# Splitting the first transposes' PSUM tile in two, so that ScalarE and VectorE copy its halves out side by side

## The chip, the cores and the metric

One NeuronCore of a Trainium2 chip runs the whole program. The metric is the device time of one execution in microseconds (us); lower is better. The spans quoted with traces run from the first to the last instruction and are about 1.7 us shorter than the time.

## The reference

Two layers are applied twice, with residual adds, to x of 2048 tokens by 1024 features in bf16:

```python
x = A_x
x = x + A(layernorm(x))     # 32 heads, window of 8 keys with dilation 2, then @ wo
x = x + B(layernorm(x))     # relu(x W_gate) * (x W_up) @ W_down, F = 3584
x = x + A(layernorm(x))
x = x + B(layernorm(x))
```

The kernel works on blocks of 512 tokens (four token tiles of 128). Only its first 15 us matter here: load block 0 of x, normalise it, transpose it so that features lie on partitions (`xnT`), and start the V projection `x @ wqkv[:, 2048:3072]` of that block.

## The kernel before

Tile 0 and 1 are normalised on VectorE; tile 2's statistics run on ScalarE at the same time. TensorE transposes a token tile in eight 128x128 pieces into one PSUM tile `tp` (128 partitions by 2 KB, one bank), and two engines copy it to SBUF, VectorE the first four pieces (`xnT[:, t, 0:4]`) and ScalarE the last four. `on("v", ...)` and `on("a", ...)` keep each engine's instructions in the order written.

```python
        def turn(t):
            tps[t] = psum.tile([P, KC, P], BF16, tag="acc", name="tp")
            for c in range(KC):
                with pe_group():
                    tail_pe[0] = nc.tensor.transpose(tps[t][:, c, :], xna[:, t, c * P:(c + 1) * P], ident[:]).ins

        def copy(t, eng, c0=0, c1=KC):
            f = nc.vector.tensor_copy if eng == "v" else nc.scalar.copy
            on(eng, f, hold["xnT"][:, t, c0:c1, :], tps[t][:, c0:c1, :])

        warm = small("warm")
        on("a", nc.scalar.activation, warm[:], ones[:, 0:1], ACT.Identity)
        scratch(14)                # 14 matmuls on ones, only to warm TensorE up
        # [cut: statistics of tiles 0 and 1 on VectorE, of tile 2 on ScalarE]
        apply(0)                   # normalise, VectorE
        turn(0)
        apply(1)
        copy(0, "v", 0, KC // 2)
        copy(0, "a", KC // 2, KC)
        turn(1)
        act_vpe(2, st1)            # three small VectorE operations for tile 2
        copy(1, "v", 0, KC // 2)
        copy(1, "a", KC // 2, KC)
        # [cut: statistics of tile 3; tiles 2 and 3 are turned and copied later, between V matmuls]
```

The V matmuls of block 0 take token tiles 0 and 1 first (256 columns), accumulating over eight feature chunks `kc`. The first four chunks need VectorE's halves, the last four ScalarE's:

```python
        plan = [(c, 0, 2) for c in range(6)] + [(c, 2, 4) for c in range(6)] + [(c, 0, 4) for c in range(6, KC)]
        # for each (c, t0, t1): for kc in range(8):
        mm(acc[:, cols], lhsT=slab[("v0", c // 4)][:, kc, (c % 4) * P:(c % 4 + 1) * P],
           rhs=ln["xnT"][:, t0:t1, kc, :], start=(kc == 0), stop=(kc == KC - 1))
```

Weights arrive in slabs of 1 MB through a ring of five; the first V slab is the fourth transfer in the SyncE queue, behind three transfers of x:

```python
        def f(key=key, src=src):
            shp = list(src.shape)
            t = wring.tile([P, 8 * SLAB], BF16, tag="slab", name=...)
            tv = t[:, 0:shp[1] * shp[2]].rearrange("p (a b) -> p a b", b=shp[2])
            sp_dma(tv, src)
            slab[key] = tv
```

## Time and profile before

| | before |
|---|---|
| time, median of the first three runs, none of them profiled | 1630.64 us (1630.27 to 1630.65) |
| profiled execution | 1630.08 us, span 1628.4 us |
| TensorE busy | 1618.6 us, 99% of the span |
| first V matmul starts | 9.69 us |
| fifth V matmul starts | 10.30 us |

This is the view of TensorE's waits of the kernel before: who waited, for whom, total us, times, longest.

```profile
PE scratch L129 <- DVE ones L296: 1.5, 1, 1.5
PE dacc L129 <- DVE x L700: 0.8, 1, 0.8
PE acc_v L129 <- DVE xnT_first L103: 0.6, 1, 0.6
PE tp L364 <- DVE xn_first L103: 0.4, 1, 0.4
```

There is nothing else in 1628 us. A change to the first transposes can act only on the third line and on what comes just after it.

Next, lines of the timeline of the kernel before, by engine: start, duration, instruction, shape, and in brackets the idle time before it and what ended it. PE is TensorE, DVE is VectorE, ACT is ScalarE.

```profile
7.45 0.62 PE L364 MATMUL tp<-ident,xn_first 128*128 128x128 bf16 x8
7.83 0.55 DVE L103 TENSOR_SCALAR xn_first<-x,mv,rstd 128x1024 bf16<-128x1024 bf16 x1 [0.45 <-POOL rstd L314]
8.30 0.42 DVE L103 COPY xnT_first<-tp 128x512 bf16<-128x512 bf16 x1
8.44 0.62 PE L364 MATMUL tp<-ident,xn_first 128*128 128x128 bf16 x8 [0.37 <-DVE xn_first L103]
...
8.75 0.58 ACT L314 COPY xnT_first<-tp 128x512 bf16<-128x512 bf16 x1 [1.62 <-DVE xnT_first L103]
...
9.22 0.41 DVE L103 COPY xnT_first<-tp 128x512 bf16<-128x512 bf16 x1
...
9.67 0.58 ACT L314 COPY xnT_first<-tp 128x512 bf16<-128x512 bf16 x1 [0.34 <-DVE xnT_first L103]
9.69 2.96 PE L129 MATMUL acc_v<-xnT_first,w_v 128*128 128x256 bf16 x24 [0.63 <-DVE xnT_first L103]
9.69 0.42 PEld L129 LDWEIGHTS <-w_v 128*128 128x128 bf16 x4 [0.75 <-issue]
10.30 2.06 PEld L129 LDWEIGHTS <-w_v 128*128 128x128 bf16 x19 [0.20 <-issue]
```

Read the two ScalarE lines. ScalarE sat idle for 1.62 us and started its copy at 8.75, just after VectorE's copy of the same token tile had ended (8.30 + 0.42). It did the same at 9.67. The two engines take turns on one PSUM tile. The last two lines (PEld) are TensorE's weight loads: four at 9.69, then a pause to 10.30, when the fifth V matmul starts. ScalarE's second half is ready just before (9.67 + 0.58).

The Trainium skill, page "PSUM — Partial Sum Buffer", section "PSUM bank collisions raise a hardware error", says that two engines must not access one bank on the same 32 partitions at once, reads included, and that the hardware does not arbitrate. So the order has to be kept by waits, and this trace shows them kept: never both engines on one tile. That the target in SBUF is not the cause is visible too: VectorE's copy of tile 1 (from 9.22) runs while ScalarE still copies tile 0 (to 9.33).

### The profile page before, as it was taken

The numbers are of one execution on the slowest core, as the hardware profiler recorded it, in microseconds if no ns is written. First come the engines' busy times: TensorE is split into PE (matmuls) and PEld (weight loads), VectorE is DVE, ScalarE is ACT, GpSimd is POOL, SyncE is SP. The second block draws the span as 40 slices with busy tenths as digits, with TensorE's granted clock in tenths as the row PEclk, the third lists the DMA queues.
The fourth block names the chain that finished last, engine by engine and source line by source line (L and its number), as shares of the span: only waits on it lengthen the run. The fifth ranks groups of instructions, "written<-read, shape, count | busy, mean of one in ns | idle before, by whom it ended". The sixth has DMA issues, their size and how long they took to land.

```text
span 1628.4 us, 18703 instructions
## 1 busy us (share of the span) xinstructions
PE 1618.6 (99%) x7589; PEld 782.2 (48%) x7638; DVE 1062.6 (65%) x926; ACT 506.1 (31%) x1050; POOL 255.7 (16%) x220
## 2 busy tenths in 40 slices
PE   9999999999999999999999999999999999999999
PEld 6644445444544445444454444544445444444444
DVE  5799899985497927949179492894818958211211
ACT  4754313243241513405134051331513311131110
POOL 2421003310250102201052010520105100000000
PEclk9999999999999999999999999999999999999999
DMA  9579656746476485664857647577484764655451
GB/s 303 93 203 252 167 177 199 192 156 200 136 215 175 155 233 171 184 175 150 229 181 185 187 150 225 162 203 212 151 231 154 194 205 155 206 164 172 156 168 65
DMA packets 371463, 296.83 MB, mean 182 GB/s; under 512 B 142512, under 2 KB 351664, under 8 KB 370480
## 3 DMA queue, kind: packets, MB, share of 16 engines
q1 hardware_dynamic: 371088, 295.23, 63.2%
q8 instruction: 60, 0.98, 0.3%
q10 hardware_dynamic: 288, 0.39, 0.1%
q14 instruction: 27, 0.22, 0.0%
HBM read 256.77 MB, written 21.00 MB: 171 GB/s over the span
## 4 chain that ended last, share of the span: by engine, by line
PE 95%; DVE 4%; issue 1%; DMA 0%; POOL 0%; DVEq 0%
PE acc_g L129 24%; PE acc_u L129 24%; PE dacc L129 22%; PE acc_v L129 7%; PE acc_k L129 6%; PE acc_q L129 6%; PE acc_wo L129 6%; DVE t L541 2%; DVE ac L551 1%; PE L L129 1%; DVE pv L603 0%; DVE x L648 0%; DVE pv L604 0%; DVE ac L541 0%; DMA x<-in_A_x_dram 0%
## 5 line engine op out<-in xcount | busy, mean ns | idle before, releaser
L129 PE MATMUL acc_g<-xnT_b,w_g 128*128 128x512 bf16 x1792 | 423.4, 379 | 0.0
L129 PE MATMUL acc_u<-xnT_b,w_u 128*128 128x512 bf16 x1792 | 423.3, 379 | 0.0
L129 PE MATMUL dacc<-w_d,hT 128*128 128x512 bf16 x1759 | 386.5, 379 | 2.5 <-DVE x L700 0.8
L672 ACT ACTIVATE r<-acc_g 128x512 bf16<-128x512 f32 x224 | 133.4, 596 | 747.1 <-PE acc_g L129 746.0
L673 DVE TENSOR_TENSOR hT<-acc_u,r 128x512 bf16<-128x512 f32 x224 | 153.7, 687 | 315.1 <-PE acc_u L129 313.5
L129 PEld LDWEIGHTS <-hT 128*128 128x128 bf16 x1792 | 175.4, 98 | 212.3 <-issue 1.0
L129 PEld LDWEIGHTS <-w_g 128*128 128x128 bf16 x1792 | 174.8, 98 | 212.7 <-issue 3.0
L129 PEld LDWEIGHTS <-w_u 128*128 128x128 bf16 x1792 | 175.4, 98 | 211.4
L541 DVE TENSOR_TENSOR t<-q,k 128x2048 f32<-128x2048 bf16 x84 | 191.7, 2290 | 8.6 <-ACT k L480 5.8
L551 DVE TENSOR_TENSOR ac<-ac,t 128x2048 f32<-128x2048 f32 x84 | 191.7, 2282 | 0.4
L485 POOL COPY kh<-k 128x14 bf16<-128x14 bf16 x64 | 81.2, 1273 | 471.9 <-ACT k L480 471.8
L700 DVE TENSOR_TENSOR x<-dacc,x 128x512 bf16<-128x512 f32 x64 | 42.5, 687 | 164.0 <-PE dacc L129 164.0
L603 DVE TENSOR_TENSOR pv<-a,vhm 128x4096 bf16<-128x4096 bf16 x64 | 145.2, 2282 | 0.0
L129 PE MATMUL acc_wo<-w_o,oT 128*128 128x512 bf16 x496 | 111.0, 379 | 0.8
L245 POOL TENSOR_TENSOR st_b<-st_b,neg_half 128x1 f32<-128x1 f32 x29 | 56.4, 1956 | 288.6 <-ACT st_b L244 288.6
L245 POOL TENSOR_TENSOR st_a<-st_a,neg_half 128x1 f32<-128x1 f32 x32 | 41.9, 1315 | 319.2 <-ACT st_a L244 319.1
L484 POOL COPY k<-kh 128x14 bf16<-128x14 bf16 x48 | 70.5, 1469 | 65.9 <-DVE t L541 43.8
L129 PEld LDWEIGHTS <-oT 128*128 128x128 bf16 x512 | 50.0, 98 | 60.4
L604 DVE TENSOR_TENSOR pv<-pv 128x2048 bf16<-128x2048 bf16 x64 | 77.4, 1215 | 0.2
L476 ACT CAST q<-acc_q 128x512 bf16<-128x512 f32 x64 | 37.3, 583 | 73.2 <-PE acc_q L129 73.2
L240 ACT ACTIVATE xn_b<-x 128x1024 bf16<-128x1024 bf16 x29 | 30.3, 1045 | 89.3 <-DVE x L648 89.3
L480 ACT CAST k<-acc_k 128x512 bf16<-128x512 f32 x64 | 37.3, 583 | 63.0 <-PE acc_k L129 62.8
(131 smaller groups left out, 1209.1 us busy)
## 6 DMA issues: line engine op xcount, KB each, us to landing
w_g<-in_B_W_gate_dram SPq DMA_DIRECT2D x56, 1024.0 KB, 7.0
w_u<-in_B_W_up_dram SPq DMA_DIRECT2D x56, 1024.0 KB, 5.4
w_d<-in_B_W_down_dram SPq DMA_DIRECT2D x48, 1024.0 KB, 5.8
w_o<-in_A_wo_dram SPq DMA_DIRECT2D x16, 1024.0 KB, 7.2
vhm<-v_d SPq DMA_DIRECT2D x32, 284.0 KB, 6.9
v_d<-vT SPq DMA_DIRECT2D x8, 1024.0 KB, 10.0
oT<-o_d SPq DMA_DIRECT2D x32, 256.0 KB, 4.4
w_d<-in_B_W_down_dram SPq DMA_DIRECT2D x16, 512.0 KB, 4.0
```

Source lines behind the costliest of these rows:

```text
L129: tail_pe[0] = nc.tensor.matmul(*args, **kwargs).ins
L245: nc.gpsimd.tensor_tensor(rstd, vpe, neg_half[:, 0:1], op=ALU.pow)
L476: tail_act[0] = nc.scalar.copy(q[:], acc[:]).ins
L484: nc.gpsimd.tensor_copy(k[:, 0:HALO], khalo[n - 1][:, c, :])
L485: nc.gpsimd.tensor_copy(khalo[n][:, c, :], k[:, BLK:BLK + HALO])
L541: nc.vector.tensor_tensor(t[:], i0, i1, op=ALU.mult)
L551: nc.vector.tensor_tensor(o, ac[:], t[:], op=ALU.add)
L603: nc.vector.tensor_tensor(tt[:], a_bc, v_sh, op=ALU.mult)
L604: nc.vector.tensor_tensor(tt[:, 0:4], tt[:, 0:4], tt[:, 4:8], op=ALU.add)
L672: tail_act[0] = nc.scalar.activation(r[:], acc[:], ACT.Relu).ins
L673: nc.vector.tensor_tensor(hold["hT"][:, j, :], accs["u"][:], r[:], op=ALU.mult)
L700: nc.vector.tensor_tensor(xs, ac[t], xs, op=ALU.add)
```

## The change

Each token tile gets two PSUM tiles of four pieces, in two banks, so the halves can be copied at the same time. The engines are also redistributed: both halves of tile 0 go to ScalarE, and the second half of tile 2 moves to VectorE.

```diff
         def turn(t):
-            tps[t] = psum.tile([P, KC, P], BF16, tag="acc", name="tp")
+            tps[t] = [psum.tile([P, KC // 2, P], BF16, tag="acc", name=f"tp{h}") for h in range(2)]
             for c in range(KC):
                 with pe_group():
-                    tail_pe[0] = nc.tensor.transpose(tps[t][:, c, :], xna[:, t, c * P:(c + 1) * P], ident[:]).ins
-
-        def copy(t, eng, c0=0, c1=KC):
+                    tail_pe[0] = nc.tensor.transpose(tps[t][c // (KC // 2)][:, c % (KC // 2), :],
+                                                     xna[:, t, c * P:(c + 1) * P], ident[:]).ins
+
+        def copy(t, eng, h):
             f = nc.vector.tensor_copy if eng == "v" else nc.scalar.copy
-            on(eng, f, hold["xnT"][:, t, c0:c1, :], tps[t][:, c0:c1, :])
+            on(eng, f, hold["xnT"][:, t, h * (KC // 2):(h + 1) * (KC // 2), :], tps[t][h][:])
 ... (cut)
-        copy(0, "v", 0, KC // 2)
-        copy(0, "a", KC // 2, KC)
+        copy(0, "a", 1)
+        copy(0, "a", 0)
         turn(1)
         act_vpe(2, st1)
-        copy(1, "v", 0, KC // 2)
-        copy(1, "a", KC // 2, KC)
+        copy(1, "v", 0)
+        copy(1, "a", 1)
 ... (cut)
-        hold["later"] = {2: (lambda: (turn(2), copy(2, "a"))),
-                         4: (lambda: (turn(3), copy(3, "v", 0, KC // 2), copy(3, "a", KC // 2, KC)))}
+        hold["later"] = {2: (lambda: (turn(2), copy(2, "a", 0), copy(2, "v", 1))),
+                         4: (lambda: (turn(3), copy(3, "v", 0), copy(3, "a", 1)))}
```

## The prediction

> **What bounds the kernel now.** TensorE. The page has PE busy 1618.6 of 1628.4 us (99%), and the view of waits lists only four PE waits in the whole run: 1.5 us for the first constant, 0.4 us for the second normalised token tile, 0.6 us before the first V matmul, 0.8 us near the end. So the change can act only on the start-up, before the first V matmul.
>
> **Start-up, from the timeline (us).** Transposes of tile 0 at 7.45, tile 1 at 8.44 (8 each, 0.61-0.62 together). DVE: normalise tile 1 at 7.83, copy (128x512) of tile 0 at 8.30, three small operations of tile 2's statistics at 8.63 to 9.15, copy of tile 1 at 9.22 (0.41). ACT: copies at 8.75 and 9.67 (0.58 each), each within 0.05 of the end of DVE's copy of the same tile, although ACT was free from 7.1. The first V matmul starts at 9.69; the fifth, which needs ACT's half, at 10.30 (0.17 later than its 0.109 step would give).
>
> ACT's copies are held because both halves lie in one PSUM tile, one bank. The Trainium skill, "PSUM — Partial Sum Buffer", section "PSUM bank collisions raise a hardware error", says two engines must not access one bank and quadrant at once, reads included. The trace agrees: never both on one tile. The SBUF target is not the cause: DVE's copy of tile 1 (9.22) overlaps ACT's of tile 0 (8.75 to 9.33).
>
> **What changes.** DVE's copy of tile 0 moves to ACT; tile 2's second half moves from ACT to DVE; the same-bank wait goes; four more PSUM slots are taken in the rotation of six.
>
> My new schedule, from those durations:
> - ACT copies tile 0: second half at 8.1, first at 8.6, done 9.18; tile 1's second half 9.10 to 9.69.
> - DVE: statistics from 8.30, tile 1's first half from 8.89 (its fourth transpose ends about 8.83, estimate from 0.219 each at 0.057 steps) to 9.31.
> - First V matmul at about 9.36 (was 9.69, gain 0.33); the fifth at 9.80, its data ready at 9.74, so the 0.17 stall goes too. Gain: 0.5 us.
>
> Later copies (tiles 2 and 3) were not waited for by PE before: nothing to gain there. PSUM rotation: each slot's previous user is, by this schedule, emptied over 1 us before it is asked for again, so no new PE wait.
>
> **Does the gain last?** PE runs on without waits for 1.6 ms, and the next weight slab and next x loads are issued when PE frees a slab (the DMA queue waited 10.9 us for PE there), so they move forward too. I expect all 0.5 us kept, or a tenth or two lost. That is 0.03%, about the width of the three runs (0.38 us).
>
> **Prediction:** 1630.15 us, range 1629.5 to 1630.75. Faster by over 2%: 0.005; within 2%: 0.99; slower by over 2%: 0.005.
>
> **What would show each step.** First V matmul 0.3 earlier, fifth 0.5 earlier; the PE wait before it about 0.3 instead of 0.6; ACT's and DVE's copies of tile 1 overlapping; first Q matmul at about 24.2 instead of 24.69; span 1627.9 instead of 1628.4.
>
> **What would make it wrong.** (1) DVE's half copy waits for all eight transposes: gain about 0.3. (2) ACT's copies start late or still serialise with DVE. (3) The slot rotation makes transposes or V matmuls wait for an eviction. (4) The early DMA, near saturated at 9 to 19 us, does not move with PE and a weight or x load is waited for at 25 to 60 us, giving the gain back. (5) A shifted DMA pattern that disturbs a later stage.

## The result, and the profile after

| | before | after |
|---|---|---|
| time, median (four runs each) | 1630.45 us (1630.27 to 1630.65) | 1630.44 us (1629.66 to 1630.48) |
| profiled execution, span | 1628.4 us | 1628.0 us |
| first V matmul | 9.69 us | 9.42 us |
| first Q matmul | 24.69 us | 24.24 us |
| last VectorE add | 1624.50 us | 1624.06 us |

Executions over 1.5% slower than the fastest of the same kernel are left out of the means. The ratio is 0.9999, with a 95% interval of 0.9981 to 1.0016. Such a ratio is the mean time of one kernel's runs over the mean of the other's of the same rounds, so it is not quite the ratio of the medians quoted.

The times do not differ, but the two traces do. These are the lines of the timeline after that answer to those of before.

```profile
7.42 0.62 PE L364 MATMUL tp<-ident,xn_first 128*128 128x128 bf16 x8 [0.37 <-DVE xn_first L103]
7.80 0.55 DVE L103 TENSOR_SCALAR xn_first<-x,mv,rstd 128x1024 bf16<-128x1024 bf16 x1 [0.45 <-POOL rstd L314]
8.07 1.58 ACT L314 COPY xnT_first<-tp 128x512 bf16<-128x512 bf16 x3 [0.86 <-PE tp L364]
8.27 0.15 DVE L103 TENSOR_SCALAR mean<-st 128x1 f32<-128x1 f32 x1
...
8.86 0.41 DVE L103 COPY xnT_first<-tp 128x512 bf16<-128x512 bf16 x1
...
9.39 2.53 PEld L129 LDWEIGHTS <-w_v 128*128 128x128 bf16 x24 [0.53 <-DMA w_v<-in_A_wqkv_dram]
9.42 2.78 PE L129 MATMUL acc_v<-xnT_first,w_v 128*128 128x256 bf16 x24 [0.39 <-DVE xnT_first L103]
```

ScalarE now starts at 8.07, released by the transposes and no longer by VectorE, and does three copies in a row; VectorE's copy of tile 1 (8.86 to 9.27) lies inside that stretch. The V matmuls run as one group of 24 in 2.78 us, where they took 2.96 us before: the pause before the fifth is gone. The weight load at 9.39 is labelled as released by the DMA of the slab `w_v`. In this trace that is loose, for the slab had landed at 8.9 (issued at 2.23, 6.7 to landing) and VectorE's copy ended later (9.27). The weight load comes equally late, 9.43, in after_half below, whose half slab had landed at 7.5; in both traces a separate wait for VectorE stands in TensorE's queue ahead of that weight load. Still, the label is a warning to keep in mind.

The chain that ended last shows where the gain goes: start and duration of each piece, here the first V matmuls, the first Q matmuls and the end. First the kernel before, then after.

```profile
10.30 2.34 PE acc_v L129 x20
...
24.85 1.73 PE acc_q L129 x8
...
1624.50 0.69 DVE x L700
```

```profile
9.42 2.78 PE acc_v L129 x24
...
24.40 1.73 PE acc_q L129 x8
...
1624.06 0.69 DVE x L701
```

The shift is 0.45 us at the first Q matmuls and 0.44 us at the last add, 1600 us later. In this pair of traces the whole gain arrives at the end. And yet the three other executions of the changed kernel, of which only times and spans exist, took 1630.44 to 1630.48 us, as long as before. The one low time of the four is the profiled one.

### The profile page after: what moved, and what is told of

It reads as the page before. It is cut to its first block, busy times and chain, and to the rows that moved or that the text cites. A ratio compares the mean times of both kernels' runs of the same rounds, so it can differ in the third digit from the quotient of the medians.

```text
span 1628.0 us, 18706 instructions
## 1 busy us (share of the span) xinstructions
PE 1618.0 (99%) x7589; PEld 782.0 (48%) x7638; DVE 1062.8 (65%) x926; ACT 506.3 (31%) x1051; POOL 256.0 (16%) x220
## 4 chain that ended last, share of the span: by engine, by line
PE 95%; DVE 4%; issue 1%; DMA 0%; POOL 0%; DVEq 0%
PE acc_g L129 24%; PE acc_u L129 24%; PE dacc L129 22%; PE acc_v L129 7%; PE acc_k L129 6%; PE acc_q L129 6%; PE acc_wo L129 6%; DVE t L542 2%; DVE ac L552 1%; PE L L129 1%; DVE pv L604 0%; DVE x L649 0%; DVE pv L605 0%; DVE ac L542 0%; DMA x<-in_A_x_dram 0%
## 6 DMA issues: line engine op xcount, KB each, us to landing
v_d<-vT SPq DMA_DIRECT2D x8, 1024.0 KB, 10.2
```

## The experiments

The theory at the start: the gain is a constant shift, worth about 0.4 us, and is passed on whole. The rivals: it is given back later, or it exists only in the profiled execution. Each kernel below ran five times, and the kernel before nine times in the same rounds on the same chip (four sessions on four chips). The first of the five executions was profiled, and it counts in the medians.

A way to read start-ups past each other was needed, since the first half tile of x lands at a slightly different time in each execution. I subtract the start of VectorE's first statistics operation, which that landing releases (3.47 to 4.59 us in these traces), from the start of the last VectorE add. For before this gives 1624.50 - 3.60 = 1620.90 us; for after, 1624.06 - 3.56 = 1620.50. I call it the length from x. All lengths come from the traces; "slab" is the issue of the first V slab plus its time to landing, the smallest in the view of that tile when it is cut to the first 10 us; it is good to 0.1 us (for the three kernels with halves it is the first half of the slab).

| kernel | x | slab | first V | last add | length from x | median time | before, same rounds |
|---|---|---|---|---|---|---|---|
| before | 3.60 | 8.7 | 9.69 | 1624.50 | 1620.90 | 1630.45 | |
| after | 3.56 | 8.9 | 9.42 | 1624.06 | 1620.50 | 1630.44 | 1630.45 |
| after_again | 3.78 | 9.6 | 9.66 | 1624.31 | 1620.53 | 1630.37 | 1630.35 |
| after_third | 3.54 | 9.3 | 9.39 | 1624.04 | 1620.50 | 1630.29 | 1630.28 |
| split_only | 3.47 | 9.4 | 9.55 | 1624.20 | 1620.73 | 1630.10 | 1630.35 |
| assign_only | 3.52 | 9.7 | 9.71 | 1624.37 | 1620.85 | 1630.30 | 1630.35 |
| late_tiles_only | 3.72 | 9.7 | 9.82 | 1624.64 | 1620.92 | 1630.23 | 1630.21 |
| late5 | 3.63 | 8.8 | 11.77 | 1629.27 | 1625.64 | 1633.71 | 1630.35 |
| late5_warm | 3.60 | 9.6 | 11.75 | 1626.40 | 1622.80 | 1632.10 | 1630.21 |
| before_wv | 4.59 | 8.9 | 10.69 | 1625.53 | 1620.94 | 1630.31 | 1630.21 |
| after_wv | 3.75 | 8.4 | 9.60 | 1624.28 | 1620.53 | 1630.22 | 1630.21 |
| before_half | 3.80 | 8.3 | 9.89 | 1624.71 | 1620.91 | 1630.10 | 1630.28 |
| after_half | 3.61 | 7.5 | 9.46 | 1624.11 | 1620.50 | 1629.55 | 1630.28 |
| after_half_again | 3.69 | 8.1 | 9.60 | 1624.24 | 1620.55 | 1629.57 | 1630.25 |

### after_again and after_third: the changed kernel, unchanged

> The changed kernel again, in five rounds beside the kernel before. Theory (the gain is a constant shift of everything after the first V matmul, and is kept to the end): the median is 0.3 to 0.5 us below that of before of the same rounds; the first V matmul of the profile starts near 9.4. Rival (the gain shows only in the one profiled pair and is given back, or is swamped by something that varies from run to run): the medians differ by under 0.15 us, or the spread of either kernel's runs is as large as the gain.

> The changed kernel once more, for more executions of the same rounds and a third trace. Theory: median 0 to 0.2 us below before, executions between 1629.6 and 1630.5 according to when the slab lands; in the trace either the slab (landing at 9.4 or later) or VectorE's copy releases the first V matmul. Rival: as before in every execution but the profiled one.

The medians were 1630.37 against 1630.35 us, and 1630.29 against 1630.28 us. So the expected 0.3 to 0.5 us did not appear in the times, a miss, while the lengths from x (1620.53, 1620.50) show 0.37 to 0.40 us of gain. The profiled execution of after_third took 1631.04 us although its last add started at 1624.04: its span ended 1.3 us later than usual, after the final stores (2.8 us to landing in the median, 2.1 in the trace of after). That is scatter at the other end of the run, and without it this execution would be about as fast as the fastest of its five (1629.74). In after_again the chain of waits before the first V matmul is no longer VectorE's copy:

```profile
2.23 7.38 DMA w_v<-in_A_wqkv_dram
9.61 0.05 issue
9.66 2.79 PE acc_v L129 x24
```

The slab was issued at 2.23 and landed at 9.61, and the matmul followed. In the traces with the full slab behind the x tiles, it landed at 8.7 to 9.7 us. The kernel before, whose copies hold V to 9.69, hardly notices that; the changed kernel, ready at 9.4, can be held by it. That gave a second theory: in the timed executions the slab's landing caps the changed kernel. In after_again itself the slab cost little (length 1620.53 against 1620.50).

### split_only and assign_only: the two parts of the change

The first has two PSUM tiles with the engines of before; the second has one PSUM tile with the engines of the change.

```diff
 split_only, against after
-        copy(0, "a", 1)
-        copy(0, "a", 0)
+        copy(0, "v", 0)
+        copy(0, "a", 1)
-        ... copy(2, "a", 0), copy(2, "v", 1)
+        ... copy(2, "a", 0), copy(2, "a", 1)

 assign_only, against before
-        copy(0, "v", 0, KC // 2)
-        copy(0, "a", KC // 2, KC)
+        copy(0, "a", KC // 2, KC)
+        copy(0, "a", 0, KC // 2)
-        ... copy(2, "a")
+        ... copy(2, "a", 0, KC // 2), copy(2, "v", KC // 2, KC)
```

> Two PSUM tiles per token tile, but the engines as before (VectorE copies the first half of tile 0, ScalarE the second). Theory: ScalarE's copies no longer wait for VectorE (first at 8.1, second at 9.05 to 9.65), but VectorE still reaches the first half of tile 1 only at 9.2, so the first V matmul stays at 9.65 to 9.7 and only the stall before the fifth goes: gain about 0.17 us of the 0.45. Rival (the split alone is what matters): gain 0.4 or more.

> One PSUM tile per token tile as before, but the engines of the change (both halves of tile 0 on ScalarE). Theory: VectorE's copy of tile 1 must wait for all eight transposes (9.06) and ScalarE's copy of tile 1 for VectorE's (9.5 to 10.1), so the first V matmul comes at about 9.5 and the fifth at about 10.14: gain about 0.16 us. Rival (taking tile 0 off VectorE is what matters): gain 0.3 or more.

The split alone behaved as calculated: length 1620.73, a gain of 0.17 us. Its timeline, the two engines' copies of tile 0 and the V matmuls:

```profile
7.97 0.59 ACT L314 COPY xnT_first<-tp 128x512 bf16<-128x512 bf16 x1 [0.62 <-PE tp L364]
8.17 0.42 DVE L103 COPY xnT_first<-tp 128x512 bf16<-128x512 bf16 x1
...
9.55 2.78 PE L129 MATMUL acc_v<-xnT_first,w_v 128*128 128x256 bf16 x24 [0.63 <-DVE xnT_first L103]
```

ScalarE copied its half of tile 0 from 7.97 while VectorE copied the other half from 8.17, so two banks do let both engines read at once, and the result was correct; but VectorE reached tile 1 no sooner, and V stood at 9.55 - 3.47 = 6.08 us after x, against 6.09 before. The assignment alone gained 0.05 us (length 1620.85), less than the 0.16 expected. There the serial turns are back (VectorE's copy of tile 1 from 9.02 to 9.44, ScalarE's at 9.48), and the start of V was released by the slab at 9.71, so 0.05 is the gain with a late slab. Without it the gain could hardly have passed 0.1: ScalarE's last half was ready at 10.07, and the fifth V matmul, 6.70 us after x in before, could not have started earlier than 6.60 here (an estimate: 10.07, plus the 0.05 us that the issue took in before, less 3.52). One more difference shows: with one tile VectorE's copy of tile 1 starts 0.66 us after that tile's first transpose (8.36 to 9.02), when all eight are done; with two tiles it starts after 0.45 (8.41 to 8.86 in after), before the last four are done. So neither part gives the 0.4 us of both: VectorE must be free early, it must not wait for the other half's transposes, and ScalarE must not wait for it. The times (medians 0.25 and 0.05 us below before) scatter too much to say more.

### late_tiles_only: two PSUM tiles for token tiles 2 and 3 alone

```diff
+            if t < 2:
+                one = psum.tile([P, KC, P], BF16, tag="acc", name="tp")
+                tps[t] = [one[:, 0:KC // 2, :], one[:, KC // 2:KC, :]]
+            else:
                 tps[t] = [psum.tile([P, KC // 2, P], BF16, tag="acc", name=f"tp{h}") for h in range(2)]
 ...
-        copy(0, "a", 1)
-        copy(0, "a", 0)
+        copy(0, "v", 0)
+        copy(0, "a", 1)
```

> Two PSUM tiles for the token tiles 2 and 3 alone; tiles 0 and 1 as before. Theory (TensorE did not wait for those copies): no gain, the first V matmul near 9.69 or at the slab's landing, medians within 0.1 us of before. Rival (the earlier copies of tiles 2 and 3 pay): 0.2 us or more.

Length 1620.92, median 1630.23 against 1630.21 us: this part gains nothing, as expected.

### late5 and late5_warm: is a late start passed on whole?

late5 issues VectorE's copy of tile 1 six times instead of once. late5_warm adds eight scratch matmuls on TensorE into the gap.

```diff
         turn(1)
+        scratch(8)                      # late5_warm only
         act_vpe(2, st1)
-        copy(1, "v", 0)
+        for _ in range(6):
+            copy(1, "v", 0)
         copy(1, "a", 1)
```

> The changed kernel with VectorE's copy of tile 1's first half issued six times instead of once (same data, right result). Each further copy costs 0.33 us by the spacing of VectorE's copies, so the first V matmul comes about 1.65 us later, near 11.05. Theory (a late start is passed on whole): the time is 1.6 to 1.7 us above that of the changed kernel, 1.15 to 1.3 above before. Rival (slack later in the run absorbs part): under 1.3 us above the changed kernel.

> The kernel with five further copies of VectorE, and eight scratch matmuls on TensorE in the gap between the transposes of tile 1 and the first V matmul. Theory (the further copies alone cost 1.65 us; the other 1.6 to 1.7 of the 3.3 measured came from TensorE's clock falling back in the 2.7 us gap, so that the first V matmuls ran at half speed): the V matmuls are 0.109 us apart from the start, the time is 1631.7 to 1632.0, 1.6 to 1.7 above the changed kernel, and the spread is small. Rival (the rest comes from elsewhere, such as weight or x loads that no longer fit): 1633.3 or more.

A copy in a row with others costs 0.46 us, not the 0.33 assumed, so V came 2.28 us later after x than in after (8.14 against 5.86), not 1.65. But late5 lost much more: 3.3 us in the median, and 5.14 us of length in the trace (against after). The timeline of late5, TensorE:

```profile
8.47 0.62 PE L364 MATMUL tp<-ident,xn_first 128*128 128x128 bf16 x8 [0.37 <-DVE mean L103]
11.77 5.28 PE L129 MATMUL acc_v<-xnT_first,w_v 128*128 128x256 bf16 x24 [2.68 <-DVE xnT_first L103]
16.85 1.01 PE L364 MATMUL tp<-ident,xn_first 128*128 128x128 bf16 x8
```

And the same trace by stretches; the columns after the bounds are the length, then busy time and count of PE, PEld, DVE, ACT and POOL, then the granted clock, the DMA share and GB/s.

```profile
8.00:10.80 2.80, 0.72 (x10) 0.45 (x8) 2.51 (x9) 1.58 (x3) 0.55 (x1) 1.00 1.10 354
10.90:17.60 6.70, 5.83 (x32) 4.27 (x33) 3.15 (x8) 1.21 (x4) 0.55 (x1) 0.50 1.05 385
17.70:22.00 4.30, 4.30 (x46) 3.91 (x45) 0.85 (x2) 2.27 (x6) 0.00 (x0) 1.00 0.39 140
```

The 24 V matmuls took 5.28 us instead of 2.78, and the granted clock was 0.50 from 10.9 to 17.6. The Trainium skill, page "TensorE: Matmul & The Clock Gate", section "Part 1: The HAM clock gate", says that the array runs at half clock after an idle window of about 3.4 us and returns to full after a busy one. The trace agrees on half the clock; the cold stretch lasted 6.8 us (the granted clock is 0.50 over all of 10.85 to 17.67), about two such windows, and TensorE had been idle for less than one before it (see the last section). late5_warm has the same VectorE work and the same late V matmul (11.75), but no cold stretch:

```profile
8.90 1.89 PE L129 MATMUL scratch<-ones 128*128 128x512 bf16 x8
11.75 1.47 PE L129 MATMUL acc_v<-xnT_first,w_v 128*128 128x256 bf16 x12 [0.96 <-DVE xnT_first L103]
```

Its length is 1622.80: 2.30 us more than after, for a V start 8.15 - 5.86 = 2.29 us later. In this trace a late start is passed on one for one. In the times it lies 1.89 us above before, where the lengths say 1622.80 - 1620.90 = 1.90. The absolute values in my expectations were wrong because the cost of a copy was; the cause of the rest of late5 is settled by this run. The times of late5 say the same: its one execution with a mean granted clock of 1.000 took 1631.92 us, as late5_warm did (1631.92 to 1632.63), and the four at 0.998 to 0.999 took 1633.67 to 1634.87.

So a start that is 2.29 us late arrives whole at the end in the trace, and within the scatter in the medians. That points to the start as the place where the timed executions of the changed kernel lose the gain; no run shows it directly.

### before_wv and after_wv: the slab ahead of the fourth x tile

```diff
+            elif t == 3:
+                pass                    # in load_x, block 0
 ...
+    sp_dma(first_view, wqkv_v[:, :, 2 * D:2 * D + SLAB])
+    sp_dma(x_tiles[3][:], x_dram[3 * P:4 * P, :])
```

> The kernel before, with the first V weight slab issued ahead of the fourth x tile instead of behind it. Theory (the slab's landing, 8.7 to 9.7 in the traces so far, is a second limit that lies just behind the old start of V and just ahead of the new one): the slab lands about 0.7 us earlier (256 KB at 370 GB/s), at 8.0 to 9.0, and the kernel before gains nothing to 0.1 us, since its copies end at 9.6. Rival (the slab's landing has no part in it): no change here and none in the next run either.

> The changed kernel with the same reordering of loads. Theory: no execution waits for the slab any more, the first V matmul always comes about 5.8 us after the first x half has landed (3.5 to 3.8), so near 9.4; the median is 0.35 to 0.5 us below that of the kernel before with the same reordering, and 0.15 to 0.3 below the changed kernel. Rival: the same as the changed kernel, within 0.1 us of before.

before_wv changed nothing, as expected; its profiled execution took 1631.12 us because x itself landed 1 us late (4.59), with a normal length of 1620.94. after_wv was a miss: 1630.22 against 1630.21 us, with the profiled execution at 1629.87 and the others at 1630.13 to 1630.56. In its trace nothing waits for the slab (8.4). Either the slab's landing is not what caps the timed executions, or moving it ahead of 256 KB is not enough, or the fourth x tile, now behind 1 MB, came late in them. No trace of an execution other than the profiled ones exists to tell. This is the one experiment that speaks against the slab theory.

### before_half, after_half and after_half_again: the slab in two halves

The first V slab is loaded as two column halves of 512 KB, with the x tiles ahead of it as before. The first V matmuls need only the first half.

```diff
-                sp_dma(tv, src)
+                if key == ("v0", 0):
+                    sp_dma(tv[:, :, 0:SLAB // 2], src[:, :, 0:SLAB // 2])
+                    sp_dma(tv[:, :, SLAB // 2:SLAB], src[:, :, SLAB // 2:SLAB])
+                else:
+                    sp_dma(tv, src)
                 slab[key] = tv
```

> The kernel before, with the first V weight slab loaded in two halves by columns (512 KB each), so that the first V matmuls need only the first half. Theory (the slab's landing, late in most timed executions at 9.4 to 9.8, caps the changed kernel and only touches the kernel before): the first half lands about 1.3 us earlier, near 8.2; the kernel before keeps its start at 9.69 (x landing plus 6.09), median within 0.15 us of before. Rival: no effect here and none in the next run.

> The changed kernel with the same halves. Theory: the cap is gone without delaying the fourth x tile (which the last reordering did), the first V matmul comes at the x landing plus 5.85 in the trace and the whole distribution moves: most executions at 1629.6 to 1630.0, the median 0.3 to 0.45 below the kernel before with the same halves. Rival (something other than the slab, not seen in the traces, holds the timed executions of the changed kernel back): median within 0.15 of before, with only the first, profiled execution low.

> The changed kernel with the slab in halves, once more on whatever chip comes. Theory (its start is held by VectorE's copy alone): median 0.5 to 0.75 us below before of the same rounds (0.45 of the change, the rest from executions of before whose slab came late), four of five executions under 1629.9; in the trace V starts 5.85 us after the first x half's statistics could begin less 0.03. Rival (the last result was luck of five executions): median within 0.2 us of before.

Now the times show the gain. after_half: 1629.59, 1629.55, 1630.29, 1629.46, 1629.35 us; before_half on the same chip: 1629.90 to 1630.21. On another chip, after_half_again gave 1629.45 to 1629.96, against 1630.05 to 1630.62 of before without the slow run. The gain expected there was 0.5 to 0.75 us, and four of five under 1629.9; it was 0.68 in the medians (1630.25 for before without the slow run), and four of five. The ten executions of the changed kernel with halves average 1629.65 us and the five of before_half 1630.09, a difference of 0.44 us (0.55 in the medians of the same chip, where 0.3 to 0.45 was expected); the lengths from x give 1620.91 - 1620.50 = 0.41. The trace of after_half has the chain that the prediction described, with VectorE's copy last:

```profile
8.98 0.34 DVE xnT_first L103
9.33 0.14 issue
9.46 2.78 PE acc_v L129 x24
```

The same edit moved the kernel before by 0.18 us (1630.10 against 1630.28), a little more than the 0.15 expected. A slab that is late in some executions could do that, but the scatter of its times is as large (0.19), and in the three traces with halves the time is 5.5 us more than the start of the last add, where it is 5.6 in the others, so some 0.1 us of it lies at the other end of the run. The ratio of after_half to before is 0.9997 (0.9983 to 1.0010), and of after_half_again 0.9996 (0.9982 to 1.0010): at that resolution neither is called faster. 9 of the 10 executions lie below 1630.0 us, against 1 of 39 of the kernel before, 1 of 5 of before_half and 4 of 14 of the changed kernel with the whole slab. It is the best of the kernels tried, by about 0.6 us in 1630.

## Why the prediction was right or wrong

- TensorE the bound ("PE busy 1618.6"), start-up the only place: right. The shift at the first Q matmuls is the shift at the end (0.45 and 0.44 us), and late_tiles_only gained nothing.
- The shared bank as the reason for ScalarE's waits: right. With two tiles ScalarE starts at 8.07 (predicted 8.1), and split_only, which changes nothing else that matters, removes the pause before the fifth V matmul and gains 0.17 us (predicted 0.17).
- The new schedule: right within 0.1 us. VectorE's copy of tile 1 came at 8.86 (8.89), ended at 9.27 (9.31), first V at 9.42 (9.36), first Q at 24.24 (24.2). The gain is 0.40 us by the length from x, not 0.5. After VectorE's copy ended the first V matmul took 0.14 us to issue, where it had taken 0.05 before, when its weights had been loaded ahead (8.84).
- "PE runs on without waits", passed on to the end: right in the traces, and late5_warm shows it one for one (2.30 of 2.29 us).
- The PSUM rotation: right, no wait for a slot appears.
- "I expect all 0.5 us kept": this is the step that failed. The gain is kept from the first V matmul to the end in the traces, but the times of most executions of the changed kernel do not have it: 10 of 14 took 1630.13 us or more, and their median is 1630.4. The likely reason, not seen in a trace, is that the sum left out the other operand: the first weight slab, whose landing I knew only to be before 8.84 in one trace, and which lies at 8.7 to 9.7 in all. My point (4) named weights, but at 25 to 60 us. Loading the slab in halves, which leaves the copies alone, brings 0.44 us of difference into the times. So the time of 1630.44 us lies inside the range (1629.5 to 1630.75) and "within 2%" was right, but the gain that the figure of 1630.15 stands for (0.3 us under before's 1630.45, or 0.5 under the first median of 1630.64) was not there. The range was wide enough for a kernel with the gain and for one without it, so that the time fell inside it says nothing for the step.

What stays open. Loading the slab in halves brings the gain into the times; that a late slab is what it removes is argued, not shown, for no slow execution was profiled. Two things speak for caution. In after, after_again, split_only, assign_only and after_wv the profiled execution is the fastest of its kernel (1629.66, 1629.91, 1629.79, 1629.95, 1629.87), and after_third's would about equal its fastest but for its late end, while most of the others took 1630.1 to 1630.5. So the profiled execution may start differently from the rest, because it is profiled or because it is the first, and the landings in the traces need not hold for the others. And an estimate: in the traces with the whole slab, after_third's late end apart, the time is 5.6 us more than the start of the last add, and in after the last add starts 1614.64 us after the first V matmul; an execution of 1630.4 us then started V near 10.2, later than any slab landed in a trace (9.7). Why the slab should land so late is not known, nor why after_wv, with its slab at 8.4 in its trace, did not help. Halving the slab also changes when the later transfers are issued, and the runs do not separate that from the earlier landing.

## What to carry to other kernels

When two operands reach an instruction by separate paths, look at the landing of both before you shorten one: here the slab landed about 0.9 us before the first V matmul in the trace of the kernel before, and 0.1 us after VectorE's copy had ended in a trace of the changed kernel (after_again). The two engines that emptied one PSUM tile took turns; here a bank for each half, and nothing else to copy first for the engine on the critical path, gave 0.4 us of length together, and neither alone did. For gains below a microsecond, compare lengths between two events of one trace, and then check that several timed executions show the same difference. Here one pair of traces showed 0.4 us that the times did not have.

## What the Trainium skill lacked or had wrong

- "TensorE: Matmul & The Clock Gate", section "Part 1: The HAM clock gate": the table says that the clock falls after at least one idle window. In late5 it fell at about 10.8 us, when TensorE had been idle for 1.7 us and had been busy for 1.32 of the 3.4 us before (sixteen transposes and the end of a matmul). A partly idle stretch was enough there, and it cost about 2.9 us (5.14 of length less the 2.28 by which V came later).
- The same page and section gives the moment of warming up a spread of 500 ns either way. The traces agree that it varies, but by more: the same 14 scratch matmuls, started at 1.52 us in each, took 4.62 to 6.10 us, a spread of 1.5 us.
- No page gives a spread for the landing of a load behind others in a queue. The same 1 MB slab, issued at 2.23 us, landed at 8.7 to 9.7 us, the first half tile of x released VectorE at 3.47 to 3.80 us and once at 4.59, and the final stores once took 1.3 us longer. Whether these make up the scatter of the kernel before's times (standard deviation 0.19 us of the 37 executions below 1631 us) was not tested.
- "PSUM — Partial Sum Buffer" was right: in split_only the two engines read two banks at once, from 8.17 to 8.56 us, with a correct result. The page has no figure for what taking turns costs; here ending it alone was worth 0.17 us of length, and 0.40 together with the move of one copy to the other engine.
